# Attention kernel with exponentials on two engines: V by column tiles, the first K and Q in halves, one warm-up run, rearranged loads, new constants for the planner

## The chip, the cores and the metric

The kernel runs on one core of a Trainium2 chip. A core has TensorE (PE, matmuls; PEld is its weight load), VectorE (DVE), ScalarE (ACT), GpSimd (POOL), and SyncE (SP), which here only issues DMAs. They run beside each other and wait for each other by semaphores. The metric is the device time of one execution in microseconds, the median over several runs.

## What is computed

Two attention layers of 16 heads of 28 over 2048 positions of width 448; their outputs stand side by side in one 896-wide result. Layer A has one K and one V for all heads (softmax over all 2048 keys); layer B has its own K and V per head and looks at 8 keys, every second position backwards.

```python
def _A_ref(x, wq, wk, wv, wo):
    q = (x @ wq).reshape(B, S, H, Dh) with heads in front
    k = x @ wk
    v = x @ wv
    scores = jnp.einsum("bhqd,bkd->bhqk", q, k) * (Dh ** -0.5)
    p = _softmax(scores, axis=-1)
    o = jnp.einsum("bhqk,bkd->bhqd", p, v)
    return o (heads side by side) @ wo
def _B_ref(x, wqkv, wo):
    q, k, v = heads of (x @ wqkv)
    idx = pos[:, None] - 2 * arange(8)[None, :]
    logits = jnp.einsum("bhsd,bhswd->bhsw", q, k[idx]) * scale, -1e9 where idx < 0
    attn = _softmax(logits, axis=-1)
    o = jnp.einsum("bhsw,bhswd->bhsd", attn, v[idx])
    return o (heads side by side) @ wo
return jnp.concatenate([a, b], axis=-1)
```

## The kernel before

The program is recorded as a list of operations, each with an engine, an estimated duration, what it reads and writes, a priority `pr` (lower goes first) and sometimes an earliest time `rel`. A planner (`Sched.run`) plays them on a clock of its own, picks for each engine the ready operation with the lowest `pr`, and so fixes the order of each engine's instructions; `resolve` then derives the semaphore waits. On the chip the engines follow that order strictly: durations and `rel` shape the order and nothing else.

Layer A. The scores are computed transposed, 128 keys by 512 queries: a unit is (query block of 512 `sc`, group of four heads `t`, key tile `tb`, head in the group `j`), 4 x 4 x 16 x 4 = 1024 units. Units are taken three and two at a time in turn into PSUM banks 0 to 2 and 3 to 4 (`SLOTS`). For each such group PE computes the scores (QK, lines 808 to 816), and ScalarE takes the exponential of the whole group in one instruction (line 833, 1536 or 1024 wide). QK has two forms: tiled, where three or two matmuls of 28 (32) rows run beside each other in row tiles (line 816), or full, where each matmul uses the whole array on a K that is zero outside its head's rows (`kz`, line 813). The planner takes the full form where its running sum of PE activity is below a bound, and puts in matmuls on a zero tile (`warm`) as fillers (lines 413, 436 and 808) to keep that sum up. For a few groups a quad, VectorE takes one unit's exponential instead of ScalarE (`d_exp`: line 912 out of PSUM into `d_x`, then the polynomial of lines 921, 923 and 925 on 1024 columns; `OFF_AT` says in which rounds). PV (line 879) multiplies the exponentials by V for four heads at a time in column tiles into bank 5; V has a column with the softmax's denominator (`v_aug`). After a quad's 64 units VectorE transposes and divides (lines 939 to 948), and after four quads PE multiplies by the output matrix (line 962). Banks 6 and 7 (`XBANKS`) serve everything else.

The head (`a_head`, `a_tr`, `a_v`, `a_q`). PE runs `WARM` matmuls on zeros (line 651). The first two blocks of 512 rows of x come in plain and are transposed on PE (line 694) and copied out (lines 702 and 705); the other two come by DMA transposes on SP. K and Q of a block are matmuls of 512 columns (lines 660 and 752) in four steps over the width; then each is squared (line 666 on ScalarE for K's first block, 758 for the first Q, VectorE otherwise), the squares are multiplied by a constant matrix into the same bank (lines 674 and 766), so that three spare rows carry the softmax's shift, and VectorE copies the bank out with a constant added (lines 677 and 770). The first QK waits for both copies. V of a block is computed as x times wv in sixteen matmuls of 28 columns (line 716) into a bank of its own, beside four one-column matmuls (line 723), whose exponential (line 727, ScalarE, `gcol`) scales V (line 731).

Layer B goes through in 16 blocks of 128 positions between these: q, k (line 1003) and v (line 1018) on PE; v is stored to DRAM and loaded back shifted, eight times (lines 1025 and 1027 on SP); products on VectorE (1044 and 1098) and sums on PE (1053 and 1104); the softmax's exponential is on ScalarE (line 1079), 256 columns for two blocks. Its first positions need zero rows in DRAM, written at line 631.

## Time and profile before

| | us |
|---|---|
| median of the runs | 452.68 (452.05 to 453.52, 4 runs) |
| the profiled execution | 452.05 |
| its span, first to last instruction | 450.0 |
| first exponential of line 833 starts | 10.83 |
| ScalarE busy, of it line 833 | 435.2, 429.7 |
| VectorE busy | 416.8 |
| PE busy (weight loads) | 418.6 (164.1) |
| mean granted PE clock | 0.999 |

Busy time is the union of an engine's instructions; a row of groups shows the line, engine and operation, what is written from what, and, after the bars, busy us, mean ns of one, and the idle time just before, with who ended it. The order of the first DMAs is: SP issues wk, then eight transposes of A's x (4.55 to 14.86), wqkv, and all sixteen of B's x (16.10 to 41.40), and then the zero rows; ACT issues the first two blocks of x and the first part of wq; POOL issues wv (2.24 and 3.14), the rest of wq (7.66 and 8.43), B's wv (8.96 and 9.72) and the two output matrices (10.25 and 12.76).

### The profile page before, as it was taken

To read this page: it belongs to the slowest core of one execution; us is meant where nothing else is said; L and a number is where in the kernel's file an instruction comes from. 1 tells how busy PE (TensorE), PEld (TensorE's weight loads), DVE (VectorE), ACT (ScalarE), POOL (GpSimd) and SP (SyncE) were. 2 spreads that over 40 slices of the span, in tenths; PEclk is the share of its full clock that TensorE was granted. 3 is DMA by queue.
4 is the path that set the end of the run, shared out by engine and by line. 5 is a ranking of instruction groups with operands and counts; after the bars stand their busy time and mean duration, and the time that the engine had idled before them with its cause. 6 is when DMAs were issued, how large, how long until landed. Compare 5 with 4: busy or idle time off the path is not lost.

```text
span 450.0 us, 9035 instructions
## 1 busy us (share of the span) xinstructions
PE 418.6 (93%) x3806; PEld 164.1 (36%) x3806; DVE 416.8 (93%) x672; ACT 435.2 (97%) x429; POOL 14.4 (3%) x37
## 2 busy tenths in 40 slices
PE   8998999898999999999899999999999899998894
PEld 3332223232344324234362353324433244442441
DVE  6778999999998999999989999999999989799972
ACT  3998999999999999999999999999999999999995
POOL 8300000000000000000000000000000000000000
PEclk9999999999999999999999999999999999999999
DMA  7994022000023002002050240002300123330001
GB/s 168 224 111 82 15 79 93 12 1 1 16 89 114 32 20 84 21 13 82 14 172 31 65 152 12 12 0 94 104 12 11 42 83 103 97 98 1 12 1 52
DMA packets 39988, 27.30 MB, mean 61 GB/s; under 512 B 15518, under 2 KB 39592, under 8 KB 39948
## 3 DMA queue, kind: packets, MB, share of 16 engines
q1 hardware_dynamic: 37452, 24.06, 19.5%
q0 software_dynamic: 816, 1.53, 1.7%
q10 hardware_dynamic: 1680, 1.13, 0.8%
q8 instruction: 30, 0.49, 0.5%
q14 instruction: 10, 0.08, 0.1%
HBM read 18.06 MB, written 5.52 MB: 52 GB/s over the span
## 4 chain that ended last, share of the span: by engine, by line
ACT 91%; DVE 5%; PE 3%; POOL 1%; issue 0%; POOLq 0%
ACT expT L833 90%; PE ps L660 1%; DVE kz L680 1%; DVE d_x L912 1%; ACT e_t L1079 1%; DVE d_u L921 1%; DVE d_u L923 1%; DVE xT_A L702 0%; PE ps L813 0%; DVE qT L770 0%; DVE kT L677 0%; PE ps L436 0%; PE ps L816 0%; DVE kT L670 0%; DVE dexp L925 0%
## 5 line engine op out<-in xcount | busy, mean ns | idle before, releaser
L833 ACT ACTIVATE expT<-ps 128x1024 bf16<-128x1024 f32 (+1 forms) x410 | 429.7, 1257 | 4.3 <-PE ps L816 2.1
L816 PE MATMUL ps<-qT,kT 32*128 32x512 bf16 (+1 forms) x918 | 130.4, 372 | 13.7 <-ACT expT L833 10.6
L879 PE MATMUL ps<-expT,v_aug 128*32 128x512 bf16 (+1 forms) x1000 | 89.8, 375 | 1.4 <-ACT expT L833 1.0
L816 PEld LDWEIGHTS ps<-qT,kT 32*128 32x128 bf16 x918 | 32.8, 91 | 101.8 <-ACT expT L833 87.0
L912 DVE TENSOR_SCALAR d_x<-ps 128x512 f32<-128x512 f32 x84 | 57.4, 684 | 2.1 <-PE ps L816 1.9
L813 PE MATMUL ps<-qT,kz 128*128 128x512 bf16 (+1 forms) x170 | 47.1, 367 | 7.1 <-ACT expT L833 5.4
L925 DVE SCALAR_TENSOR_TENSOR dexp<-d_u,d_x 128x1024 int16<-128x1024 f32 x42 | 51.2, 1218 | 0.1
L923 DVE SCALAR_TENSOR_TENSOR d_u<-d_u,d_x 128x1024 f32<-128x1024 f32 x42 | 51.2, 1218 | 0.1
L921 DVE SCALAR_TENSOR_TENSOR d_u<-d_x 128x1024 f32<-128x1024 uint16 x42 | 51.1, 1216 | 0.2
L1044 DVE TENSOR_TENSOR stage<-qTB,kTB 112x1024 bf16<-112x1024 bf16 x64 | 42.3, 677 | 1.0 <-PE ps L1053 0.9
L1104 PE MATMUL ps<-ident,prod 128*112 128x128 bf16 x512 | 42.2, 224 | 0.0
L1098 DVE TENSOR_TENSOR prod<-Vsh,a_n 128x896 bf16<-128x896 bf16 x64 | 37.6, 616 | 4.7 <-PE ps L1104 4.7
L1003 PE MATMUL ps<-xT_B,wqkv 128*128 128x512 bf16 x128 | 39.0, 383 | 0.7 <-DVE qT L770 0.4
L879 PEld LDWEIGHTS ps<-expT,v_aug 128*32 128x32 bf16 x1000 | 22.1, 93 | 47.9 <-issue 43.1
L1104 PEld LDWEIGHTS ps<-ident,prod 128*112 128x112 bf16 x512 | 34.0, 129 | 14.7 <-issue 11.7
L1053 PEld LDWEIGHTS ps<-ones,stage 112*128 112x128 bf16 x512 | 19.9, 96 | 9.2 <-issue 4.3
L1053 PE MATMUL ps<-ones,stage 112*128 112x4 bf16 x512 | 22.9, 167 | 0.0
L752 PE MATMUL ps<-xT_A,wq 128*128 128x512 bf16 x64 | 19.6, 383 | 0.4 <-DVE kTB L1008 0.2
L813 PEld LDWEIGHTS ps<-qT,kz 128*128 128x128 bf16 x170 | 10.9, 97 | 24.0 <-ACT expT L833 21.1
L1018 PE MATMUL ps<-wqv,xT_B 128*128 128x448 bf16 x64 | 18.1, 356 | 0.9 <-DVE kTB L1008 0.5
L1111 PE MATMUL ps<-wo_B,oT 112*128 112x448 bf16 x64 | 18.3, 357 | 0.0
L962 PE MATMUL ps<-wo,oTn 128*128 128x448 bf16 x64 | 16.5, 355 | 1.1 <-DVE oTn L948 1.1
(105 smaller groups left out, 304.0 us busy)
## 6 DMA issues: line engine op xcount, KB each, us to landing
Vsh<-v_scratch SPq DMA_DIRECT2D x16, 896.0 KB, 4.7
v_scratch<-Vst SPq DMA_DIRECT2D x16, 112.0 KB, 1.7
out_dram<-outB SPq DMA_DIRECT2D x16, 112.0 KB, 1.7
out_dram<-outA SPq DMA_DIRECT2D x15, 112.0 KB, 1.7
stage<-in_A_x_dram ACTq DMA_DIRECT2D x2, 448.0 KB, 4.2
wqkv<-in_B_wqkv_dram SPq DMA_DIRECT2D x1, 672.0 KB, 9.6
wo_B<-in_B_wo_dram POOLq DMA_DIRECT2D x4, 98.0 KB, 5.9
wo<-in_A_wo_dram POOLq DMA_DIRECT2D x4, 98.0 KB, 6.7
```

The source lines that it names most:

```text
L813: r = e.matmul(g.bank(b0 + i, nq, nq * k), g.kz[:, j, 128 * tb:128 * tb + 128], g.qT[:, sc % 2, t, q0:q0 + nq], start=True, stop=True)
L816: r = e.matmul(g.bank(b0 + i, nq, nq * k), g.kT[32 * j:32 * j + 32, 128 * tb:128 * tb + 128], g.qT[32 * j:32 * j + 32, sc % 2, t, q0:q0 + ...
L833: x = a("act", t_exp(w), lambda e, b0=b0, w=w, n=n: e.activation(g.expT[:, n % ERING, 0:w], g.ps[:, 512 * b0:512 * b0 + w], ACT.Exp, scale ...
L879: x = e.matmul(g.bank(PVBANK, nq, q0, p0=32 * j, p1=32 * j + 32), g.v_aug[:, w, tb, :], src[:, nq * k:nq * k + nq], start=first, stop=last ...
L912: o = a("dve", t_dve_ps(512), lambda e: e.tensor_scalar(out=xx[:, 512 * h:512 * h + 512], in0=g.bank(bank), scalar1=-128.0 * A2, scalar2=1 ...
L921: a("dve", t_dve_1x(1024), lambda e: e.scalar_tensor_tensor(out=u, in0=lo, scalar=EP * F, in1=lo, op0=ALU.add, op1=ALU.mult), R=di, W=["d_ ...
L923: a("dve", t_dve_1x(1024), lambda e: e.scalar_tensor_tensor(out=v, in0=u, scalar=EQ * F * F, in1=lo, op0=ALU.add, op1=ALU.mult), R=["d_u"] ...
L925: a("dve", t_dve_1x(1024), lambda e: e.scalar_tensor_tensor(out=out, in0=v, scalar=EL / F ** 3, in1=xx, op0=ALU.mult, op1=ALU.subtract), R ...
L1003: a("pe", t_mm(512), lambda e, u=u, t=t, kt=kt, w=w: e.matmul(g.bank(u.bank), g.wqkv[:, kt, w * D + KC * t:w * D + KC * t + 128], g.xT_B[: ...
L1044: op = a("dve", t_dve_2x(1024), lambda e, t=t, qv=qv, kv=kv: e.tensor_tensor(out=g.prodT[0:KC, t, :, :], in0=qv, in1=kv, op=ALU.mult), R=R ...
L1053: r = e.matmul(g.bank(u.bank, 128).rearrange("p (h w) -> p h w", w=WIN)[:, 4 * t:4 * t + 4, w], g.prodT[0:KC, t, w, :], g.ones4[:, :], sta ...
L1104: a("pe", 0.056, lambda e, u=u, t=t, w=w: e.matmul(g.bank(u.bank, 128, 128 * t, p1=KC), g.prod2[:, w, KC * t:KC * t + KC], g.ident[:, :], ...
```

## The change

- V is computed transposed: per step over the width one group of four column tiles (32 columns each, `wv4` is wv padded to 32), 128 columns long, so 16 matmuls in four groups a block; VectorE transposes the bank (`vT`) and scales it out of SBUF. The one-column matmuls of line 723 now write into the bank of the block's K, which stays in use until their exponential is done.
- K's first block and the first Q are computed, squared, corrected and copied in two halves of 256 columns; the first QK's need only their own half of K (`key_of`). The copy of K's first half goes before the copies of x.
- The warm-up is one operation of eight matmuls and one of a single matmul.
- The zero rows come from the `warm` tile and are stored early on SP; the memset of `Vst` is gone. B's x is transposed in blocks as before, but blocks 2 and 3 stand later in SP's order. The rest of wq is issued earlier on POOL, B's wv and both output matrices later.
- `d_x` has three buffers instead of two, `outA` two instead of four; the polynomials have a priority by quad instead of a fixed one; in the first quad the offload begins in round 4 instead of 7.
- The planner's constants are new: window, bounds, the activity credited to tiled operations, and a small extra duration after a change of tiling mode.

On the engines' orders this gives 20 full QK groups instead of 76 (of 410), 35 single filler matmuls instead of 23, and 14 fillers inside other operations instead of 42. ScalarE keeps its exponentials: 288 of 1024, 121 of 1536 and one of 512.

```diff
-WARM = 9
+WARM = 8
+KF = 256
...
-OFF_AT[0] = (7, 8, 9, 10)
+OFF_AT[0] = (4, 5, 6, 7)
 LATE = 2
-PSTT = -1.5
+PSTT = -35.0
 DR = 2
+DX = 3
...
-    MODE = 0.09
+    MODE = 0.096
     NPV = 3
-    WIN = 2.2
-    WANT = 1200.0
-    IDLE = 1300.0
-    FULL = {2: 1500.0, 3: 1200.0}
-    LOW = 900.0
-    QKT = 0.315
+    WIN = 2.5
+    WANT = 1300.0
+    IDLE = 1400.0
+    FULL = {2: 1400.0, 3: 1300.0}
+    LOW = 1200.0
+    QKT = 0.32
...
+                elif mode and not o.tiled:
+                    o.dur += o.extra
...
-        self.outA = sb([128, 4, D], BF16, "outA")
+        self.outA = sb([128, 2, D], BF16, "outA")
...
+        a("dve", 0.1, lambda e: e.memset(g.wv4[:, :, :], 0.0), W=["wv4z"], pr=-6.5)
...
-        a("gp", 1.5, wload(g.wq, g.A_wq, KC, D), R=[("d_x", 0, 0), ("d_x", 0, 1)], W=[("wq", 1)], dsem="i_wq", land=4, pr=-7.5, ninc=2)
+        a("gp", 1.5, wload(g.wq, g.A_wq, KC, D), R=[("d_x", 0, 0), ("d_x", 0, 1)], W=[("wq", 1)], dsem="i_wq", land=5.5, pr=-8.15, ninc=2)
...
-                    transpose=True)), R=[("xst", 0)], W=[("xT_B", c, t)], dsem=f"i_xb{c}.{t}", land=4.5, pr=-16 + c)
+                    transpose=True)), R=[("xst", 0)], W=[("xT_B", c, t)], dsem=f"i_xb{c}.{t}", land=6.0, pr=-16 + c, rel=(0, 0, 60, 130)[c])
...
-        a("sp", 0.6, one(lambda e: e.dma_start(out=g.v_dram[0:PAD, :], in_=g.Vst[0:PAD, 0, :])),
-          R=[("Vst", 0)], W=[("vd", -1)], dsem="i_vz", land=2.5, pr=3, rel=4)
+        a("sp", 0.6, one(lambda e: e.dma_start(out=g.v_dram[0:PAD, :], in_=g.warm[0:PAD, 0:D])),
+          R=["warm"], W=[("vd", -1)], dsem="i_vz", land=2.5, pr=-24)
...
+        a("dve", 0.1, lambda e: e.tensor_copy(out=g.wv4[:, :, 0:DH], in_=g.wv[:, :, :]), R=["wv", "wvz", "wv4z"], W=["wv4"], pr=-5)
...
+        for n, pr, rel in ((WARM, -30, 0.0), (1, -15, 4.6)):
+            def warm(e, n=n):
+                for _ in range(n):
+                    r = e.matmul(g.bank(3), g.warm[:, 0:128], g.warm[:, :], start=True, stop=True)
+                return r
...
+            for k, (lo, n) in enumerate(((0, KF), (KF, 512 - KF)) if c == 0 else ((0, 512),)):
+                u = Use(f"K{c}.{k}", HB, late=c == 0)
...
-            g.a_v(c)
+            g.a_v(c, u)
...
+        u = Use(f"V{c}", g.LB)
+        for kt in range(4):
+            def vm(e, u=u, kt=kt):
+                for i in range(4):
+                    r = e.matmul(g.bank(u.bank, 128, 0, 32 * i, 32 * i + 32), g.wv4[:, kt, :],
+                                 g.xT_A[:, kt, 512 * c:512 * c + 512].rearrange("p (t i e) -> p i t e", t=4, e=32)[:, i],
+                                 start=kt == 0, stop=kt == 3, tile_position=(0, 32 * i))
+                return r
+            o = a("pe", 0.13, vm, R=[("xT", c, kt), "wv4"], W=[u], use=u, pr=pr, rel=11.0 if c == 0 else 0, dense=192)
+            o.tiled = True
+        a("dve", t_dve_ps(128), lambda e, u=u: e.transpose(out=g.vT[:, c % 2, :], in_=g.bank(u.bank, 128)),
+          R=[u], W=[("vT", c % 2)], use=u, pr=-2)
+        u = uk
...
+            for hf, (lo, n) in enumerate(((0, 256), (256, 256)) if first and t == 0 else ((0, 512),)):
+                pr += 0.1 * hf
+                u = Use(f"Q{sc}.{t}.{hf}", banks, late=first and t == 0)
...
-            o.dense = 128
+            o.dense = 256 + 32 * len(us)
...
-        xx, out = g.d_x[:, m % 2, :], g.dexp[:, m % DR, :]
+        xx, out = g.d_x[:, m % DX, :], g.dexp[:, m % DR, :]
...
+            pp = 10.0 + 26.7 * (4 * g.quad[0] + g.quad[1]) + PSTT
...
-            ob = blk % 4
+            ob = blk % 2
```

## The prediction

> **What bounds the kernel now.** I read the page first (engine shares, the chain that ended last), then ScalarE by shape, then its waits, then the timeline of the head, and last the stretches.
>
> ```profile
> PE 418.6 (93%) x3806; PEld 164.1 (36%) x3806; DVE 416.8 (93%) x672; ACT 435.2 (97%) x429; POOL 14.4 (3%) x37
> ...
> ACT 91%; DVE 5%; PE 3%; POOL 1%; issue 0%; POOLq 0%
> ```
>
> Three engines are above 90%, but the chain that ended last is 91% ScalarE: the exponentials of line 833, one behind the other. By shape:
>
> ```profile
> L833 ACT ACTIVATE expT<-ps 128x1024 bf16<-128x1024 f32 x288 | 291.6, 1134 | 2.1 <-PE ps L813 1.5 <-PE ps L879 0.7
> L833 ACT ACTIVATE expT<-ps 128x1536 bf16<-128x1536 f32 x121 | 188.3, 1556 | 2.1 <-PE ps L816 2.1
> ...
> L833 ACT ACTIVATE expT<-ps 128x512 bf16<-128x512 f32 x1 | 0.8, 767 | 0.0
> ```
>
> The means times the counts (288 x 1.134 + 121 x 1.556 + 0.8 = 516) exceed the 429.7 busy us of the group, so neighbours overlap by about 0.2 us each, and a wait shorter than that overlap never shows as idle. What does show is little, and where it lies is the point:
>
> ```profile
> 17.95 5.97 ACT L833 ACTIVATE expT<-ps 128x1536 bf16<-128x1536 f32 x5 [0.18 <-PE ps L816]
> ...
> 32.61 5.12 ACT L833 ACTIVATE expT<-ps 128x1024 bf16<-128x1024 f32 x5 [0.66 <-PE ps L879]
> 37.87 0.17 ACT L727 ACTIVATE gcol<-ps 128x4 f32<-128x4 f32 x1 [0.15 <-PE ps L723]
> 39.53 6.46 ACT L833 ACTIVATE expT<-ps 128x1024 bf16<-128x1024 f32 x6 [1.49 <-PE ps L813]
> ```
>
> This is ScalarE's timeline: start, length, and in brackets the idle time before. The four sum to 2.48 us, all before 40 us. The stretches (us; then busy time of PE, PEld, DVE, ACT, POOL; clock) agree that nothing is idle later:
>
> ```profile
> 31.95:39.53 7.58, 5.92 (x57) 2.33 (x61) 7.58 (x11) 5.29 (x6) 0.20 (x1) 1.00 0.51 83
> ...
> 45.00:100.00 55.00, 51.85 (x405) 16.47 (x403) 54.63 (x82) 55.00 (x55) 0.00 (x0) 1.00 0.13 41
> 100.00:200.00 100.00, 94.86 (x802) 34.71 (x799) 97.83 (x149) 100.00 (x99) 0.00 (x0) 1.00 0.13 43
> ...
> 444.30:450.00 5.70, 1.60 (x13) 0.42 (x13) 2.15 (x5) 0.54 (x1) 0.00 (x0) 0.88 0.12 40
> ```
>
> So the 450.0 us are a head of 10.83 (to the first exponential), a loop of 433.4 (to 444.2), and a tail of 5.8. The head ends like this:
>
> ```profile
> 8.59 0.75 DVE L770 TENSOR_SCALAR qT<-ps,cols 128x512 bf16<-128x512 f32 x1 [2.15 <-PE ps L766]
> 8.97 0.39 PE L674 MATMUL ps<-d_u,hq 128*128 128x512 bf16 x1
> 9.26 0.41 DVE L702 COPY xT_A<-ps 128x512 bf16<-128x512 bf16 x1
> 9.59 0.74 DVE L677 TENSOR_SCALAR kT<-ps,cols 128x512 bf16<-128x512 f32 x1
> 10.39 0.39 PE L816 MATMUL ps<-qT,kT 32*128 32x512 bf16 x3 [0.58 <-DVE kT L677]
> 10.83 5.97 ACT L833 ACTIVATE expT<-ps 128x1536 bf16<-128x1536 f32 x5 [1.91 <-PE ps L816]
> ```
>
> Q's and K's corrections are one 512-wide pass each, with a copy for the next x block between them on VectorE.
>
> **What the Trainium skill says.** "TensorE: Matmul & The Clock Gate", section "What's actually happening": the array runs at half rate until one free-running activity window of about 3.4 us was busy, and falls back after an idle one. The trace agrees: seven warm-up matmuls from 1.25 to 4.42 us at 0.43 us each, later ones at 0.21, and a granted clock of 0.88 in the thin last stretch. Same page, section "Measured speedup vs the span model": column tiles run beside each other (2.38 times for three). Four tiles of line 879 start together and the group takes 0.39 us, like one matmul. "TensorEngine Tiling", section "Key Properties": a change of tiling mode drains the array; at 10.71 and 11.03 us a weight load stands idle 0.23 us just at such changes. "DMA: Bandwidth & Descriptors", section "Issuing engines are not separate DMA queues": all queues share the 16 DMA engines, so what POOL issues earlier competes with ACT's loads; the stretch 10.83 to 18 shows a DMA share of 1.17.
>
> **The change part by part**, against the profiled run: 452.05 us, span 450.0, so 2.05 around it, which I keep. The median of the four runs shown is 452.68.
>
> *Head.* Warm-up: the old seven already run without a gap (7 x 0.43 = 3.0 of the 3.17), so one long run of eight brings no heat that was lacking; it ends near 1.25 + 8 x 0.43 = 4.69 instead of 4.42, and the transposes that began at 4.58 may lose 0.1. VectorE, busy from 3.2 to 6.4 us but for short issue gaps, gets one more small memset (0.1) and the wq copy (0.26) ahead of the x copies: the last x copy ends near 6.55 instead of 6.44, and Q's last matmul of the first half starts at 6.6. Halves of 256: pitch 0.11, end 6.87; ScalarE square (0.60 at 512; about 0.38 at 256) 6.93 to 7.31; hq matmul behind five K matmuls, 7.47 to 7.74; qT halves (0.75 at 512; about 0.43 at 256) 7.8 to 8.65; K's first half squared 7.6 to 8.0, its hq matmul behind two transposes to 8.45; kT first half 8.65 to 9.1, with no copy in between. QK needs only that half: 9.15, and the first exponential 0.45 later as before: 9.6. POOL's rest of wq (294 KB) is issued some 4 us earlier, beside the second x block, which landed at 2.72 + 4.7 = 7.4; its transposes stand in PE's queue ahead of K's hq matmul at 8.0. A slip of 0 to 1 us costs 0 to 0.4; I take 0.1. First exponential 9.7: minus 1.1 (bounds -1.4 to -0.5). The zero-row store is one issue (0.6) on SP ahead of transposes that wait for x at 4.55 anyway: nothing. wv4's copy waits on VectorE for wv (issued 3.14, 4.3 to land: 7.44), with qT queued behind it until 7.8: 0.3 of cover, and any slip beyond it goes one to one into the head.
>
> *Early loop.* Q's and K's halves take four banks (0 to 3), and K's last one is now kept for the column of line 723 and its exponential. The second pair's banks are 3 and 4, so its QK stands behind that small exponential; the order on ScalarE shows 1536, gcol, 1536, 1024: the third group overtakes the second. That third one needs the first exponential's banks: after it ends, a warm matmul (0.22), the QK (0.39) and the release (0.06) pass: idle 0.7. Second bubble: chunk 1's kT. VectorE has, from the end of kT's second half at 9.5, four x copies (4 x 0.36), three wq copies (0.8), four kz (4 x 0.36), vT (0.3 by the slope of STREAM_TRANSPOSE, 0.44 at 256 and 0.71 at 512), two v_aug (0.45), the K copy 0.68, the product 0.41, another vT, the hq matmul and 0.75: about 16.5, against 15.4 before. Chunk 0 lasts 16 of 5 units a round, 3.2 rounds of 2.23 us, plus the bubble: to 16.2. Idle 0.6 (0 to 1.5). The old four waits belong to K3, V's sixteen 28-wide matmuls a chunk with fillers, and Q of t=1 behind the offload's polynomials. V becomes four column-tile groups a chunk (16 x 0.13 = 2.1 us of PE for 64 x 0.06 + 13 fillers x 0.15 = 5.8), Q's copies get VectorE before the polynomials, and K3's, V3's and Q's products stand earlier in the order. I leave 0.4 for remnants. Sum 1.7 for 2.48: minus 0.8 (bounds -2.0 to +0.8). POOL's later loads of wqv, wo_B and wo free DMA in 10 to 18 us; B's late x waits on SP behind B's first V stores, 40 us or more before it is used: nothing.
>
> *Rest of the loop.* The order has 20 full-array QK groups instead of 76, 35 filler matmuls for 23, 14 inner fillers for 42, and 47 more entries into tiled mode. In PE time: 56 x 0.1 and 28 x 0.15 and V's 3.7 saved, 47 x 0.1 and 12 x 0.22 added: 6 us less of 418.6. PE was not the bound, and the clock was already 1.00. A loop without any wait would be about 424 (121 pairs at 2.23, 167 exponentials of 1024 at 0.90, eight of 0.3 for e_t), an estimate from the runs of exponentials above, so about 6 us of waits hidden under the overlap exist to be won or doubled. I take 0, with -1.5 to +2. DVE: a third d_x buffer and polynomials ordered by quad, 42 x 3 x 1.22 us unchanged: nothing unless a QK waits for its bank's reader, which is what these bounds hold. Two outA buffers: each is rewritten long after its 1.7 us store.
>
> *Tail.* The last exponential is 512 wide; three output matmuls (0.56) stand before the last PV and end about 0.1 after it: +0.1.
>
> Sum: -1.1 - 0.8 + 0 + 0.1 = -1.8. Profiled 450.25; median 452.68 - 1.8 = **450.9**.
>
> **Rivals.** *A, the head's gain is returned in the bubbles* (the same): if wv, wq or kT of chunk 1 are a microsecond later than worked out, -1.1 in the head stands against +0.8 in the loop: 452.4. For it: the two new bubbles are sure by bank and order. Against it: the old 1.49 and 0.66 lose their causes. *B, the clock falls* (slower): with full-array QKs gone, PE runs thin in places. The thinnest is after chunk 2's K matmuls: QK 3 and 2, one PV group, one hq, QK 2, so five streams of 512 (2560 columns) while ScalarE works some 3.3 us, a third of full rate. Before shows 1.00 at a PE busy share of 5.92/7.58 and a fall at 1.60/5.70; a third lies near the fall. One half-rate window of 3.4 us puts 1.7 us of PE work late, and beside a PE at 97% it is not caught up. It decides from two windows in a run: -1.8 + 3.4, so 454.3. Against it: the windows are free-running, so a short thin patch seldom fills one. *C, the hidden waits shrink* with the lighter PE: -1.5 more, 449.4; this is the low end of my forecast.
>
> **How the numbers follow.** This kernel's runs spread by 0.3%, so 0.2% (0.9 us) is about what can be told from no change. Forecast with C 0.66, A 0.17, B 0.17. The range: 449.0 (C and a slightly better head) to 453.0 (A with 0.6 above it); B is left out but for its edge. Faster (below 451.8) 0.68 with the lower edge of A; same 0.14; slower (above 453.6) 0.18.
>
> **What would show it.** First exponential at 9.4 to 10.0; a 0.7 idle behind the first exponential, another near 16.5; no idle at 32 and 38; 100.00 of 100 us busy later; clock 1.00 to the tail, and QK matmuls of 0.39 in every stretch. Wrong would be a first exponential after 10.4, matmuls of 0.6 in mid-loop, or a loop from first to last exponential above 433.4.

## The result, and the profile after

The changed kernel takes 451.13 us in the median of 43 runs (449.21 to 466.87), the kernel before 452.68 in 64; the ratio is 0.996, with a 95% interval of 0.9948 to 0.9972. Ratios leave out slow runs, more than 1.5% above the fastest of their kernel: here the four from 456.76 on, further down the two above 500 of experiment 2 and the two longest of experiment 4. The forecast was 450.9. The profiled run took 451.95 us, with a span of 450.2.

The median hides something. The 43 runs do not scatter, they stand on steps, and the mean granted clock of TensorE stands on the same steps:

| runs | time, us | mean clock |
|---|---|---|
| 12 | 449.21 to 449.75 | 0.996 to 0.998 |
| 12 | 450.57 to 451.60 | 0.992 to 0.995 |
| 6 | 451.94 to 452.01 | 0.990 to 0.991 |
| 9 | 452.95 to 453.60 | 0.987 to 0.988 |
| 4 | 456.76 to 466.87 | 0.976 and below |

A stretch of 3.41 us at half rate lowers the mean clock of a 450 us run by 3.41 x 0.5 / 450 = 0.004, so one step is one such stretch. The kernel before has steps too, of about 0.6: its fastest runs, at 452.04 to 452.13, have a clock of 0.998 or 0.999, those around its median, near 452.6, one of 0.996. Its traced run, at 452.05, is of the fastest, so where the clock falls in the others is not on record.

The changed kernel's profiled run is of the third group and has two stretches. Its page first: busy time by engine, the clock in 40 slices, and the chain that ended last.

```profile
PE 419.3 (93%) x3800; PEld 159.0 (35%) x3800; DVE 419.3 (93%) x680; ACT 435.2 (97%) x431; POOL 14.0 (3%) x36
...
PEclk9999999999999999999999989989999999999999
...
ACT 94%; PE 3%; POOL 1%; DVE 1%; issue 0%; POOLq 0%
```

The chain is still ScalarE, one exponential behind the other. What is new are the two slices with an 8 in the clock, the 24th and the 27th, in mid-loop. ScalarE's timeline (start, length, idle time before in brackets), first the early loop:

```profile
10.06 1.45 ACT L864 ACTIVATE expT<-ps 128x1536 bf16<-128x1536 f32 x1 [1.18 <-PE ps L847]
11.41 0.17 ACT L754 ACTIVATE gcol<-ps 128x4 f32<-128x4 f32 x1
12.33 4.62 ACT L864 ACTIVATE expT<-ps 128x1536 bf16<-128x1536 f32 x4 [0.75 <-PE ps L847]
17.44 2.36 ACT L864 ACTIVATE expT<-ps 128x1024 bf16<-128x1024 f32 x2 [0.49 <-PE ps L847]
...
31.64 18.89 ACT L864 ACTIVATE expT<-ps 128x1024 bf16<-128x1024 f32 x18
```

The waits at 18, 32, 38 and 39 us are gone, two new ones stand at 12.33 and 17.44, and no other follows up to 50. The same view in the middle, where before had no idle time:

```profile
265.20 1.02 ACT L864 ACTIVATE expT<-ps 128x1024 bf16<-128x1024 f32 x1 [0.41 <-PE ps L844]
266.72 1.02 ACT L864 ACTIVATE expT<-ps 128x1024 bf16<-128x1024 f32 x1 [0.49 <-PE ps L844]
...
296.12 1.02 ACT L864 ACTIVATE expT<-ps 128x1024 bf16<-128x1024 f32 x1 [0.51 <-PE ps L844]
297.63 1.02 ACT L864 ACTIVATE expT<-ps 128x1024 bf16<-128x1024 f32 x1 [0.49 <-PE ps L844]
```

ScalarE waits for full-array QK matmuls. The stretches (start and end, length, then busy time of PE, PEld, DVE, ACT, POOL, then the clock) say why:

```profile
45.00:100.00 55.00, 53.06 (x415) 16.15 (x413) 54.65 (x82) 55.00 (x55) 0.00 (x0) 1.00 0.12 29
100.00:200.00 100.00, 95.35 (x844) 36.33 (x842) 98.13 (x149) 100.00 (x99) 0.00 (x0) 1.00 0.21 58
...
260.79:264.20 3.41, 2.64 (x27) 1.06 (x27) 3.41 (x7) 3.41 (x4) 0.00 (x0) 1.00 0.30 91
264.20:267.61 3.41, 3.41 (x20) 1.48 (x18) 3.04 (x6) 2.51 (x3) 0.00 (x0) 0.50 0.63 212
...
291.51:294.92 3.41, 2.36 (x15) 0.69 (x15) 3.41 (x7) 3.41 (x5) 0.00 (x0) 1.00 0.00 0
294.92:298.33 3.41, 3.41 (x11) 0.69 (x9) 2.00 (x5) 2.41 (x3) 0.00 (x0) 0.50 0.00 0
```

Each half-rate stretch is exactly 3.41 us long and follows a stretch of the same length in which PE was busy 2.64 or 2.36 us. PE did not stop for a whole window there; it ran tiled matmuls with gaps, the longest 0.62 and 0.90 us. In the half-rate stretches a full-array matmul of 512 columns takes 0.61 to 0.63 us instead of 0.38, and ScalarE falls from 3.41 busy to 2.51 and 2.41.

Waits shorter than the overlap of two exponentials never show as idle time. To count them too, I took every pair of neighbours on ScalarE and set the distance of their starts against the pace back to back (0.904 us for 1024 columns, 1.331 for 1536, and 0.05 and 0.30 for a small exponential of `gcol` or `e_t` between two, from the runs of exponentials in the trace). What is above that pace, by place:

| us lost | before | after, profiled |
|---|---|---|
| first exponential starts | 10.83 | 10.06 |
| up to 20 us | 0.39 | 1.61 |
| 20 to 45 us | 3.01 | 0.13 |
| after 45 us | 5.34 | 7.50, of it 1.78 and 1.74 in the two half-rate stretches |
| last exponential's end to the span's end | 5.75 | 5.96 |

The head gained 0.77 and the early loop 3.40 - 1.74 = 1.66, and the tail lost 0.21. If the two stretches' 3.52 were simply taken out, the loop after 45 us would have gained 5.34 - 3.98 = 1.36. The runs say less. Those at 449.22, which have no stretch in the loop, have a span of 447.5, against 450.0 of before's traced run, which has none either: 2.5 gained, so 0.3 is left for the loop after 45 us. (The trace of experiment 1, without a stretch too, loses 4.82 there, 0.5 less than before.) And the runs with two stretches stand 2.73 above those with none (451.95 against 449.22), not 3.52: part of what a stretch costs in place is won back later. How is not shown.

So undisturbed against undisturbed the gain is 452.05 - 449.22 = 2.8 us, of which 0.3 lies outside the span (2.05 around it before, 1.7 now). In the median run 1.9 of it is given back. Before's median in turn stands 0.6 above its undisturbed runs, so that the medians differ by 1.55.

### The profile page after: what moved, and what is told of

Same layout as the page of the kernel before. It is cut to its first block, busy times and chain, and to the rows that moved or that the text cites. A ratio compares the mean times of both kernels' runs of the same rounds, so it can differ in the third digit from the quotient of the medians.

```text
span 450.2 us, 9037 instructions
## 1 busy us (share of the span) xinstructions
PE 419.3 (93%) x3800; PEld 159.0 (35%) x3800; DVE 419.3 (93%) x680; ACT 435.2 (97%) x431; POOL 14.0 (3%) x36
## 4 chain that ended last, share of the span: by engine, by line
ACT 94%; PE 3%; POOL 1%; DVE 1%; issue 0%; POOLq 0%
ACT expT L864 93%; PE ps L844 1%; ACT e_t L1111 1%; PE ps L847 1%; PE ps L994 0%; PE ps L910 0%; PE ps L781 0%; DVE qT L800 0%; POOL wqkv L572 0%; POOL wv L601 0%; PE ps L1136 0%; POOL d_x L601 0%; PE ps L796 0%; POOL wv L602 0%; PE ps L675 0%
## 5 line engine op out<-in xcount | busy, mean ns | idle before, releaser
L847 PE MATMUL ps<-qT,kT 32*128 32x512 bf16 (+1 forms) x1043 | 151.8, 371 | 18.1 <-ACT expT L864 13.3
L910 PE MATMUL ps<-expT,v_aug 128*32 128x512 bf16 (+1 forms) x1000 | 95.2, 377 | 0.0
L847 PEld LDWEIGHTS ps<-qT,kT 32*128 32x128 bf16 x1043 | 37.9, 91 | 116.7 <-ACT expT L864 104.8
L1136 PE MATMUL ps<-ident,prod 128*112 128x128 bf16 x512 | 46.4, 227 | 0.1
L910 PEld LDWEIGHTS ps<-expT,v_aug 128*32 128x32 bf16 x1000 | 24.1, 93 | 53.3 <-issue 50.4
L1035 PE MATMUL ps<-xT_B,wqkv 128*128 128x512 bf16 x128 | 40.3, 386 | 0.1
L1085 PEld LDWEIGHTS ps<-ones,stage 112*128 112x128 bf16 x512 | 18.6, 96 | 10.0 <-issue 5.9
L781 PE MATMUL ps<-xT_A,wq 128*128 128x512 bf16 (+1 forms) x68 | 20.3, 371 | 0.3 <-DVE wq L645 0.3
L844 PE MATMUL ps<-qT,kz 128*128 128x512 bf16 (+1 forms) x45 | 14.5, 418 | 2.9 <-ACT expT L864 2.7
L971 DVE STREAM_TRANSPOSE PV_T<-ps 128x512 f32<-128x512 f32 (+1 forms) x17 | 11.6, 681 | 5.8 <-PE ps L910 5.7
```

The source lines that it names most:

```text
L847: r = e.matmul(g.bank(b0 + i, nq, nq * k), g.kT[32 * j:32 * j + 32, 128 * tb:128 * tb + 128], g.qT[32 * j:32 * j + 32, sc % 2, t, q0:q0 + ...
L910: x = e.matmul(g.bank(PVBANK, nq, q0, p0=32 * j, p1=32 * j + 32), g.v_aug[:, w, tb, :], src[:, nq * k:nq * k + nq], start=first, stop=last ...
L1035: a("pe", t_mm(512), lambda e, u=u, t=t, kt=kt, w=w: e.matmul(g.bank(u.bank), g.wqkv[:, kt, w * D + KC * t:w * D + KC * t + 128], g.xT_B[: ...
L1085: r = e.matmul(g.bank(u.bank, 128).rearrange("p (h w) -> p h w", w=WIN)[:, 4 * t:4 * t + 4, w], g.prodT[0:KC, t, w, :], g.ones4[:, :], sta ...
L1136: a("pe", 0.056, lambda e, u=u, t=t, w=w: e.matmul(g.bank(u.bank, 128, 128 * t, p1=KC), g.prod2[:, w, KC * t:KC * t + KC], g.ident[:, :], ...
```

## Experiments

Twelve kernels. Where nothing else is said, a diff is against the first experiment, which is the changed kernel with fillers enough to keep the clock in most runs, so that half-rate stretches blur the rest less.

**1. Is it the clock-keeping?** The changed kernel with the planner's old window and bounds and the old credit for QK and PV (its durations stay the new ones). The edit touches the rules for filler and full-array matmuls only, but the planner then orders everything anew: of VectorE's 678 instructions that can be compared 239 stand at the same place as in the changed kernel, of ScalarE's 430 all but 16.

```diff
-    WIN = 2.5
-    WANT = 1300.0
-    IDLE = 1400.0
-    FULL = {2: 1400.0, 3: 1300.0}
-    LOW = 1200.0
+    WIN = 2.2
+    WANT = 1200.0
+    IDLE = 1300.0
+    FULL = {2: 1500.0, 3: 1200.0}
+    LOW = 900.0
...
-            o.dense = 256 + 32 * len(us)
+            o.dense = 128
...
-            {(k, y[3], z[0] // 4) for k in ("v_aug", "v_aug1") for y in grp for z in g.parts(y[0])}), pr=-40, dense=768)
+            {(k, y[3], z[0] // 4) for k in ("v_aug", "v_aug1") for y in grp for z in g.parts(y[0])}), pr=-40, dense=700)
```

> The changed kernel with the old activity rules alone (WIN 2.2, WANT 1200, IDLE 1300, FULL 1500/1200, LOW 900, a tiled QK credited with 128 and a PV with 700 columns); head, V, loads and priorities stay changed, and the order has 69 full QK groups instead of 20. Theory clock: the changed kernel loses what lies above 449.2 us to windows of 3.41 us at half clock, about 1 to 1.7 us each, which come where the array streams too little. With the old rules there are none: 449.2 to 449.8, clock 0.998 in every run, no QK or PV of 0.6 us, and first exponential at 10.0 to 10.1 as in the changed kernel. Theory late PE: the half-rate windows only go along with QKs that are late because tiled groups were taken for cheaper than they are; with the full groups back PE is as full as before and the hidden waits return: 450.5 to 451.5.

Measured: 449.43 (449.41 to 451.24, 7 runs), ratio 0.9938 [0.9916, 0.996]. Five of the seven lie within 0.11 us of each other; the other two, at 451.15 and 451.24, have a clock of 0.994 and so a stretch each, which I had not expected. The stretches of its trace at the same two places:

```profile
264.20:267.61 3.41, 3.41 (x38) 1.81 (x36) 3.41 (x5) 3.41 (x5) 0.00 (x0) 1.00 0.40 129
294.92:298.33 3.41, 3.41 (x26) 1.23 (x25) 3.41 (x6) 3.41 (x4) 0.00 (x0) 1.00 0.00 0
```

Full clock, ScalarE without a gap, and no other half-rate stretch in the loop. The steps of the changed kernel are the half-rate stretches, and its order with the new constants has far more of them: 31 of 43 runs have one, against 4 of the 40 of experiments 1, 3, 5, 6 and 10, which all have the old constants. The constants alone do not keep the clock: experiments 4 and 9 have the old ones too, and at least 16 of the 22 runs of the one and seven of the 14 of the other have a stretch. What counts is the order that comes out of them.

**2. No clock-keeping at all.** The changed kernel with every bound at zero, so that the planner puts in no fillers for the clock and chooses no full-array QK for it.

```diff
-    WANT = 1300.0
-    IDLE = 1400.0
-    FULL = {2: 1400.0, 3: 1300.0}
-    LOW = 1200.0
+    WANT = 0.0
+    IDLE = 0.0
+    FULL = {2: 0.0, 3: 0.0}
+    LOW = 0.0
```

> The changed kernel with all bounds of the activity rules at zero: no filler matmul and no full QK group at all, nothing else changed; PE has some 17 us less to do. Theory clock: ten to fifteen windows of 3.41 us at half clock, each 1.0 to 1.7 us late: 460 to 475 us, clock 0.94 to 0.96, and matmuls of 0.6 us in stretches that begin on a grid of 3.41 us. Theory late PE: less work on PE leaves fewer late QKs: 448 to 449.5, with a clock not below 0.99.

Measured: 489.5 and 490.85, with clocks of 0.859 and 0.854, and 502.8 and 504.94, with 0.825 and 0.819; the median of the four is 496.82, and the ratio 1.0825 [1.0783, 1.0868] is that of the first two. The profile is of the 504.94. The sign is the clock theory's; the size is far above what I gave it. The late-PE theory, which had 448 to 449.5 here, is refuted; what less work on PE would be worth at full clock can't be seen in this kernel. Its page (clock by slice) and one of its stretches:

```profile
PEclk9879985999557555897999999998969895575886
```

```profile
161.06:205.43 44.37, 44.33 (x272) 13.23 (x268) 30.19 (x50) 31.43 (x30) 0.00 (x0) 0.50 0.12 38
```

44.37 us at half rate, thirteen windows of 3.41, with PE busy from end to end and ScalarE busy 31.43. PE's busy time is full, and still the clock does not come back. A fall can last.

**3. The bubble behind the first exponential.** The four one-column matmuls go into V's bank instead of K's, so that bank 3 is free once kT is copied.

```diff
-        u = uk
...
-                g.bank(u.bank, 1, b), g.kT[0:32, 128 * tb:128 * tb + 128], g.e30[:, :], start=True, stop=True),
+                g.bank(u.bank, 1, 128 + b), g.kT[0:32, 128 * tb:128 * tb + 128], g.e30[:, :], start=True, stop=True),
...
-        a("act", 0.2, lambda e, u=u: e.activation(gc, g.bank(u.bank, 4), ACT.Exp, scale=SCALE),
+        a("act", 0.2, lambda e, u=u: e.activation(gc, g.bank(u.bank, 4, 128), ACT.Exp, scale=SCALE),
```

> As e1_oldthr, but the one-column matmuls of line 750 go into columns 128 to 131 of V's own bank instead of the bank of K, so that bank 3 is free once kT's second half is copied. Theory banks: the idle 0.75 us behind the first exponential comes from bank 3 being held until the column's exponential is done; here the second exponential follows the first without idle time, and the idle time before 20 us is below 0.4. V's banks are held longer instead, and about 0.7 to 1.0 of idle time is expected near 38: 449.0 to 449.6. Rival: the idle time has another cause (the overtaking third group, the filler in front of it) and stays at 0.7: then 449.5 to 450.3, since the wait near 38 comes on top.

Measured: 449.21 (448.96 to 449.46, 6 runs), ratio 0.9921 [0.99, 0.9941]. ScalarE's timeline:

```profile
10.13 4.63 ACT L863 ACTIVATE expT<-ps 128x1536 bf16<-128x1536 f32 x4 [1.19 <-PE ps L846]
14.65 0.18 ACT L753 ACTIVATE gcol<-ps 128x4 f32<-128x4 f32 x1
...
39.47 6.03 ACT L863 ACTIVATE expT<-ps 128x1024 bf16<-128x1024 f32 x6 [0.82 <-PE ps L909]
```

Four exponentials, 1536 and 1024 wide in turn (the row names the shape of the first), run on from the first, so the bank was the cause of the 0.75. The second bubble, 0.49 at 17.44, goes with it. In the changed kernel it looks like this:

```profile
16.04 0.75 DVE L692 TENSOR_SCALAR kT<-ps,cols 128x512 bf16<-128x512 f32 x1 [0.65 <-PE ps L689]
...
17.00 0.11 PEld L847 LDWEIGHTS ps<-qT,kT 32*128 32x128 bf16 x5 [0.63 <-ACT expT L864]
17.01 0.60 PE L847 MATMUL ps<-qT,kT 32*128 32x512 bf16 x5
...
17.44 1.02 ACT L864 ACTIVATE expT<-ps 128x1024 bf16<-128x1024 f32 x1 [0.49 <-PE ps L847]
```

K of chunk 1 (`kT`) is there at 16.79. What released QK at 17.00 is an exponential of 1024 that ended at 16.95, just before this one of 1024, on the same two banks: once the third group has overtaken the second, two of these stand one behind the other. In experiment 3 the widths alternate, kT is there at 16.79 too, and this is what is left, a wait for kT:

```profile
16.84 0.10 PEld L846 LDWEIGHTS ps<-qT,kT 32*128 32x128 bf16 x3 [0.52 <-DVE kT L692]
...
17.28 2.37 ACT L863 ACTIVATE expT<-ps 128x1536 bf16<-128x1536 f32 x2 [0.18 <-PE ps L846]
```

Another wait of 0.82 appears at 39 us, as expected, and the gain over experiment 1 is 0.2.

**4. The loads.** The changed kernel with the old order of the loads (and the planner's old constants). The diff shows a part; `Vst`'s memset on POOL is back too.

```diff
-        a("gp", 1.5, wload(g.wq, g.A_wq, KC, D), R=[("d_x", 0, 0), ("d_x", 0, 1)], W=[("wq", 1)], dsem="i_wq", land=5.5, pr=-8.15, ninc=2)
+        a("gp", 1.5, wload(g.wq, g.A_wq, KC, D), R=[("d_x", 0, 0), ("d_x", 0, 1)], W=[("wq", 1)], dsem="i_wq", land=4, pr=-7.5, ninc=2)
...
-          R=["warm"], W=[("vd", -1)], dsem="i_vz", land=2.5, pr=-24)
+          R=[("Vst", 0)], W=[("vd", -1)], dsem="i_vz", land=2.5, pr=3, rel=4)
...
-          W=["wqv"], dsem="i_wbv", land=8, pr=-7, rel=15, ninc=2)
+          W=["wqv"], dsem="i_wbv", land=5, pr=-7, ninc=2)
```

> As e1_oldthr, with the loads as in the kernel before (rest of wq late on POOL, B's wv and the output matrices early, zero rows from Vst after all of B's x). Theory neutral: the moved loads hide nothing on the path, 449.2 to 449.8, first exponential 9.9 to 10.1. Rival collision: the early rest of wq takes DMA time from the second x block, whose transposes stand before K's correction on PE, so undoing it brings the first exponential 0.1 to 0.4 earlier; or the early POOL loads slow the transposed x of block 2 and K of block 2 waits for a DMA between 15 and 17: later by 0.3 to 1.

Measured: 453.2 (450.18 to 458.45, 22 runs), ratio 0.9994 [0.9979, 1.0009]. This doesn't price the loads: the moved loads change the whole order, its profiled run has half-rate stretches at 46.06 and 383.98, and its times scatter as after's do. What it does show is a head 0.30 shorter (9.76). The cause is on VectorE and POOL. The timeline of the changed kernel:

```profile
3.74 0.77 POOL L601 DMA_DIRECT2D d_x<-in_A_wq_dram  x1
4.51 0.55 POOL L602 DMA_DIRECT2D d_x<-in_A_wq_dram  x1
5.04 0.87 POOL L572 MEMSET wqkv<- 64x896 bf16 x1
5.21 0.84 DVE L640 COPY wk<-wk 128x448 bf16<-128x448 bf16 x1
5.96 0.30 DVE L645 COPY wq<-d_x 128x448 bf16<-128x448 bf16 x1
6.18 0.73 DVE L725 COPY xT_A<-ps 128x512 bf16<-128x512 bf16 x2
```

and of experiment 4:

```profile
5.01 0.47 POOL L574 MEMSET wqv<- 64x448 bf16 x1
5.20 0.40 DVE L641 COPY wk<-wk 128x448 bf16<-128x448 bf16 x1
```

In both, wk's copy ends 0.12 to 0.14 us after the memset that was running when it began (6.05 against 5.91; 5.60 against 5.48), while wq's copy of the same shape takes 0.26 to 0.30. All 14 traces agree: in the nine with the long memset there wk's copy takes 0.83 or 0.84, in the five with the short one 0.38 to 0.51, and it always ends 0.12 to 0.14 behind the memset. The copy waits for POOL. wq's rest, issued from 3.74 to 5.06 on POOL, pushed POOL's longest memset from 3.9 to 5.04, beside wk's copy.

**5 and 6. wq's rest issued late, alone.** The same kernel twice.

```diff
-        a("gp", 1.5, wload(g.wq, g.A_wq, KC, D), R=[("d_x", 0, 0), ("d_x", 0, 1)], W=[("wq", 1)], dsem="i_wq", land=5.5, pr=-8.15, ninc=2)
+        a("gp", 1.5, wload(g.wq, g.A_wq, KC, D), R=[("d_x", 0, 0), ("d_x", 0, 1)], W=[("wq", 1)], dsem="i_wq", land=4, pr=-7.5, ninc=2)
```

> As e1_oldthr, with the rest of wq issued on POOL after the memsets, as in the kernel before; from the second exponential on the order is the same but for a few DVE and PE places before 13 us. Theory port: in the changed kernel the copy that spreads wk (line 640) takes 0.84 instead of 0.51 us because POOL's memset of wqkv (line 572), pushed later by the two issues of wq, runs at the same time; here the copy takes 0.40 to 0.52, the first exponential starts at 9.7 to 9.8 instead of 10.1, and the kernel takes 449.1 to 449.2 against 449.4. Theory DMA: the early wq delays the second x block; then the copy stays at 0.84 and the first exponential comes earlier only where PE's transposes at 8.4 no longer wait. Rival: the 0.3 us comes back as a longer wait for chunk 1's K near 16, 449.4.

> The kernel m_wqlate again, since its first exponential at 10.46 came with a first full-rate window at 7.02 us, against 6.11 in e1_oldthr and 4.78 in the changed kernel, so that head and clock were mixed. Theory port: the copy of wk again takes 0.38 to 0.41 us, and where full rate begins before 6.2 us the first exponential is at 9.7 to 9.9; the time is 449.1 to 449.4 in such runs. Rival: the copy's 0.45 us are not on the path, and the first exponential is at 10.0 or later whatever the clock.

Measured: 449.84 (449.72 to 450.22, 5 runs), ratio 0.9941 [0.9929, 0.9954], and 449.76 (449.06 to 451.8, 11 runs), ratio 0.9925 [0.9896, 0.9955], against 449.43 for experiment 1. wk's copy takes 0.39 in both, as it should, and with full rate early, in the second, the first exponential comes at 9.60, a little before the 9.7 to 9.9 of the port theory. Yet nothing is gained in the time: only three of the 11 runs of experiment 6 lie below 449.4. In the first profile PE came to full rate at 7.02 us only, and the first exponential at 10.46. In the second, full rate came at 4.19 and the first exponential at 9.60; then this (VectorE's and ScalarE's timeline):

```profile
13.34 0.46 DVE L645 COPY wq<-d_x 128x448 bf16<-128x448 bf16 x2 [1.91 <-DMA d_x<-in_A_wq_dram]
...
14.42 0.31 DVE L745 STREAM_TRANSPOSE vT<-ps 128x128 f32<-128x128 f32 x1
```

```profile
15.39 2.37 ACT L864 ACTIVATE expT<-ps 128x1536 bf16<-128x1536 f32 x2 [1.17 <-PE ps L847]
```

VectorE stands 1.91 us at wq's copy, whose load came late; V's transpose is queued behind it, PE's V matmuls behind that, and QK behind those. The early issue buys cover for this and pays with the memset.

**7. K and Q in one piece.**

```diff
-KF = 256
+KF = 512
...
-            for hf, (lo, n) in enumerate(((0, 256), (256, 256)) if first and t == 0 else ((0, 512),)):
+            for hf, (lo, n) in enumerate(((0, 512),)):
```

> As e1_oldthr, with K's first block and the first Q whole again (one 512-wide pass each). Theory halves: the first exponential comes at 10.7 to 10.9, 0.7 later than with halves, since the correction, square and copy are one 0.6 to 0.75 us step each again; the idle time behind the first exponential does not go with them, and the kernel takes 450.2 to 450.9. Rival: what the halves gain in the head is given back behind the first exponential, so undoing them costs nothing: 449.3 to 449.7.

Measured: 451.72 (451.56 to 455.16, 15 runs), ratio 0.9983 [0.997, 0.9996]: 2.3 above experiment 1, more than I had given it. The first exponential starts at 11.28 instead of 10.13, and the early loop changes its order with it: idle times of 0.43 and 0.91 us come back at 22.49 and 32.29 (2.20 lost between 20 and 45, by the count of the table above, for 0.34). In this profile full rate came at 6.88, in experiment 1's at 6.11, so not all of the 1.15 is the halves'.

**8. V by sixteen matmuls a block in a bank of its own, as before.** The edit also moves the one-column matmuls into V's bank and gives V its old place in the order (a priority of 1.3 for 0.5); the diff shows a part.

```diff
...
-            o = a("pe", 0.13, vm, R=[("xT", c, kt), "wv4"], W=[u], use=u, pr=pr, rel=11.0 if c == 0 else 0, dense=192)
-            o.tiled = True
-        a("dve", t_dve_ps(128), lambda e, u=u: e.transpose(out=g.vT[:, c % 2, :], in_=g.bank(u.bank, 128)),
-          R=[u], W=[("vT", c % 2)], use=u, pr=-2)
...
+        u = Use(f"V{c}", g.LB, spare=160)
+        for b in range(4):
+            tb = 4 * c + b
+            for kt in range(4):
+                o = a("pe", 0.07, lambda e, u=u, b=b, tb=tb, kt=kt: e.matmul(
+                    g.bank(u.bank, DH, 32 * b), g.xT_A[:, kt, 128 * tb:128 * tb + 128],
+                    g.wv[:, kt, :], start=kt == 0, stop=kt == 3),
...
```

> As e1_oldthr, with V of a block computed as before, sixteen matmuls of 28 columns and a bank of its own with the one-column matmuls. Theory V: the column tiles take some 3.7 us of PE out of the first 37 us, and this is what removed the idle 0.66 and 1.49 us of the kernel before near 32 and 38; with the old V more than 1 us of idle time comes back between 20 and 40, while the 0.75 behind the first exponential goes because bank 3 is free: together 449.8 to 450.8. Rival priorities: the waits near 32 and 38 went because Q's copies now go before the polynomials; then the idle time from 20 to 40 stays below 0.5 and the kernel is as fast or faster, 448.7 to 449.4.

Measured: 451.49 (451.36 to 452.38, 16 runs), ratio 0.9977 [0.997, 0.9985]: 2.1 above experiment 1, more than I had given it. ScalarE's timeline has the old pattern again:

```profile
23.58 0.17 ACT L750 ACTIVATE gcol<-ps 128x4 f32<-128x4 f32 x1 [0.52 <-PE ps L746]
...
30.36 0.17 ACT L750 ACTIVATE gcol<-ps 128x4 f32<-128x4 f32 x1 [0.41 <-PE ps L746]
30.98 1.02 ACT L860 ACTIVATE expT<-ps 128x1024 bf16<-128x1024 f32 x1 [0.44 <-PE ps L843]
32.83 4.62 ACT L860 ACTIVATE expT<-ps 128x1536 bf16<-128x1536 f32 x4 [0.82 <-PE ps L906]
```

These are waits for V's chain and the QK behind it. V as it is in the changed kernel removes them; what of it the column tiles do and what V's earlier place in the order does was not separated.

**9. The offload's rounds in the first quad, as before.**

```diff
-OFF_AT[0] = (4, 5, 6, 7)
+OFF_AT[0] = (7, 8, 9, 10)
```

> As e1_oldthr, with the first quad's offload in rounds 7 to 10 as in the kernel before instead of 4 to 7. Theory place: the polynomials of the first quad then fall on Q of t=1 to 3, and ScalarE waits for the second quad's QK near 38 for 1.5 to 2.5 us, as the kernel before did (1.49 idle): 451 to 452. Rival: with V by column tiles and Q's copies ahead of the polynomials this place no longer matters: 449.3 to 449.8.

Measured: 452.8 (452.54 to 455.35, 14 runs), ratio 1.0003 [0.9978, 1.0028]: 3.4 above experiment 1. That is more than I had given it, but at least seven of the 14 runs have a half-rate stretch. Six without one, at 452.54 to 452.56 with a clock of 0.997 or 0.998, stand 3.1 above experiment 1, and that is the price of this part, the largest of one part. ScalarE's timeline:

```profile
37.97 1.45 ACT L864 ACTIVATE expT<-ps 128x1536 bf16<-128x1536 f32 x1 [0.64 <-PE ps L844]
41.10 4.20 ACT L864 ACTIVATE expT<-ps 128x1024 bf16<-128x1024 f32 x4 [1.68 <-PE ps L844]
```

2.3 us of idle time are where before had its 0.15 and 1.49, and one half-rate stretch at 36.42 lies on them; how much of the 1.68 is that stretch's can't be read off this trace.

**10. Seven warm-up matmuls instead of eight.**

```diff
-WARM = 8
+WARM = 7
```

> As e1_oldthr, with seven matmuls in the warm-up run instead of eight (3.0 instead of 3.4 us of heat). Theory nothing: the head is the same within the place of the first full-rate window, 449.2 to 449.9. Rival heat: the eighth carries the array over to the transposes; without it the first full-rate window comes one window (3.4 us) later in some runs, and these runs are 0.5 to 1 us longer, with a first exponential after 10.6.

Measured: 449.44 (449.4 to 451.1, 11 runs), ratio 0.9923 [0.9897, 0.9948]; the first exponential starts at 10.06. The eighth matmul is worth nothing that can be seen.

**11. The same number of full groups, placed by another measure.** The changed kernel, with a tiled matmul credited by its share of the array (a QK of two at 256, PV at 512), and bounds that leave 21 full groups for after's 20.

```diff
-    WANT = 1300.0
-    IDLE = 1400.0
-    FULL = {2: 1400.0, 3: 1300.0}
-    LOW = 1200.0
+    WANT = 1200.0
+    IDLE = 1250.0
+    FULL = {2: 1200.0, 3: 1100.0}
+    LOW = 1000.0
...
-            o.dense = 256 + 32 * len(us)
+            o.dense = 128 * len(us)
```

> The changed kernel with the activity credited by the share of the array that a matmul fills (tiled QK 128 columns a unit, PV 512, V group 128, 98 and 10 for B's sums) and bounds WANT 1200, IDLE 1250, FULL 1200/1100, LOW 1000; the order keeps 21 full QK groups (20 in the changed kernel), 31 single fillers (35) and has 37 inner fillers for 14. Theory clock, in the form that the traces so far give (windows of 3.41 us that stream less than about 850 full-array columns a us turn into a half-rate window, 35% of full): nearly the same filling work at other places removes the half-rate windows in most runs: 449.2 to 449.8, a median at clock 0.997 or above, at most one run in five with a half-rate window. Theory full groups: it is the 49 more full QK groups of e1_oldthr that keep the clock, so with 21 the spread of the changed kernel stays, median 450.5 to 451.5.

Measured: 449.67, ratio 0.9925 [0.9901, 0.995]. Six of 13 runs lie at 449.09 to 449.19, one at 449.67, six at 450.48 to 450.84. The last six have a clock of 0.993 or 0.994. So no run has more than one half-rate stretch, where 19 of after's 43 have two or more, with as few full groups: it is not the 49 more full groups of experiment 1 alone that keep the clock. The order has 37 fillers inside other operations for 14, though, so whether their place or their number helps is not separated. And six runs of thirteen still have a stretch, more than I had expected; the measure is not sharp.

**12. The parts that helped, together.** Against experiment 1: the column matmuls in V's bank (experiment 3), wq's rest late but with the planner told its true landing time (5.5 instead of 4), V earlier in the order, and LOW at 850.

```diff
-    LOW = 900.0
+    LOW = 850.0
...
-        a("gp", 1.5, wload(g.wq, g.A_wq, KC, D), R=[("d_x", 0, 0), ("d_x", 0, 1)], W=[("wq", 1)], dsem="i_wq", land=5.5, pr=-8.15, ninc=2)
+        a("gp", 1.5, wload(g.wq, g.A_wq, KC, D), R=[("d_x", 0, 0), ("d_x", 0, 1)], W=[("wq", 1)], dsem="i_wq", land=5.5, pr=-7.5, ninc=2)
...
-    VPR = 0.5
-    VP0 = 0.5
+    VPR = 0.3
+    VP0 = 0.1
```

> A version put together from the findings: old activity rules (LOW 850), the column of line 749 in V's bank, the rest of wq late on POOL, V's priority 0.3 and 0.1 instead of 0.5. Both theories add up here: first exponential at 9.7 to 9.8, idle time before 45 us below 0.7 instead of 1.3, no half-rate window: 448.2 to 448.8. Rival: one half-rate window now and then (the thinnest stretch of the order lies just at the share where the clock fell), 449.3 to 450.3 in such runs.

Measured: **447.98** (447.49 to 448.32, 4 runs), ratio 0.9897 [0.9884, 0.9911]; it beats both kernels. ScalarE's timeline:

```profile
10.36 4.63 ACT L863 ACTIVATE expT<-ps 128x1536 bf16<-128x1536 f32 x4 [0.88 <-PE ps L846]
...
14.96 2.37 ACT L863 ACTIVATE expT<-ps 128x1536 bf16<-128x1536 f32 x2
17.51 2.36 ACT L863 ACTIVATE expT<-ps 128x1536 bf16<-128x1536 f32 x2 [0.18 <-PE ps L846]
...
33.05 17.54 ACT L863 ACTIVATE expT<-ps 128x1024 bf16<-128x1024 f32 x17
```

The time is below what I had expected, although the first exponential came later, at 10.36 for 9.7 to 9.8; full rate began only at 7.09 in this profile. From the first exponential on 0.18 us of idle time are left in the loop. VectorE now does V's first transpose (13.39) before wq's copies (13.63), so the wait of experiment 6 is gone. The four edits were not tried one by one beyond experiments 3, 5 and 6.

Not tried: four `outA` buffers again, and the third `d_x` buffer and the new polynomial priorities apart from the rest.

## Why the prediction was right

The number, -1.8 to 450.9, holds within 0.23 us, and that is luck. Undisturbed the change gains 2.8, one more than forecast, chiefly because the early loop's term was too small. The half-rate stretches, which the sum put at nothing, take 1.9 of it back in the median run, and before's median, from which the forecast starts, has 0.6 above its own undisturbed runs. The traced run, forecast at 450.25, took 451.95. Of the three signs of being wrong that the prediction named two came in it: full-array matmuls of 0.61 to 0.63 us in mid-loop, and 434.2 us from the first exponential to the end of the last, above 433.4. Point by point:

- *Head: first exponential at 9.7.* It was 10.06: -0.77 for -1.1, inside the bounds. The step that failed is "the last x copy ends near 6.55": it ended at 6.91. From there on the working holds: the first exponential follows the last x copy by 3.15 us in after, 3.19 in experiment 4 and 3.17 in experiment 6. I had counted wq's early issue against DMA time and not against POOL's own order, where it pushes a memset beside wk's copy. The Trainium skill, "SBUF — State Buffer", section "SBUF: two separate sides", states that GpSimd and a VectorE instruction in a two-port mode share a port pair that one of them holds for a whole instruction while the other blocks; the trace agrees (wk's copy 0.84 for 0.40, ending 0.14 behind the memset), though it does not show the copy's mode.
- *Warm-up: at most 0.1.* Right (experiment 10).
- *Two new bubbles, 0.7 and 0.6.* The first is right in size and cause: 0.75, and experiment 3 confirms the bank. The second is 0.49, but not for the cause given: QK did not wait for chunk 1's K, which was there at 16.79, but for the two banks of the exponential before it, until 16.95 (experiment 3). The sum for it does not hold either: a first exponential at 9.7, 3.2 rounds of 2.23 and a bubble of 0.7 end at 17.5, not at 16.2, and with a kT at 16.5 that leaves no wait. That the size came near was luck.
- *The old four waits go, 0.4 remain: -0.8.* The direction is right, and experiments 8 and 9 show that the new way and place of V and the offload's rounds are what removes them (2.1 and 3.1 us come back, together more than the 2.48 of visible idle time, so the two prices do not add). The term is too small: the early loop as a whole gained 1.66. I priced visible idle time only; before lost 3.01 between 20 and 45 us by the pace of the exponentials, of which 2.30 showed, and 0.13 was left of it, not 0.4.
- *Rest of the loop: 0.* In undisturbed runs it gained 0.3 to 0.5; with the profiled run's two stretches it lost 2.2. So 0 was near for the waits and wrong for the clock. Rival C's 1.5 more from hidden waits did not come: that undisturbed runs stand near its 449.4 is the early loop's doing. PE's busy time did not fall by the 6 us worked out: it is 419.3 for 418.6, of it about 3.4 from the two half-rate stretches, an estimate from their 6.82 us of full PE time at half rate.
- *Tail: +0.1.* It was +0.2.
- *Rival B.* Its price of 1.7 was right in place (1.74 to 1.78 us a stretch); in the runs the steps are 1.8, 0.95 and 1.05 apart, less than 1.7 from the second on. Its place was wrong (not behind chunk 2's K matmuls, but at 264 and 295 in the profiled run), and so was the argument against it, that a short thin patch seldom fills a window: with some 130 windows in a run it takes one that does, and 31 of the 43 runs have at least one. It should not have been a rival with 0.17 but a term of the sum, near +1.9.
- *Rival A.* The head's gain was not returned in the bubbles. The two bubbles are there, and the early loop gained in spite of them.

So the changed kernel is worth 2.8 us undisturbed, and the order that the new clock constants give costs 1.7 to 1.9 of it in the median run: experiment 1, which undoes only these, runs at 449.43, and the undisturbed runs of the changed kernel at 449.22.

## What to carry to other kernels

Where one engine runs back to back, compare the distance of its instructions' starts with its own pace, not only the idle time: of the 8.7 us that the kernel before lost by its own pace, 2.5 showed as idle. When times of one kernel fall on steps, look at the clock before anything else, and treat filler that keeps a clock as paid by the worst window, not by the mean. Of an instruction moved earlier on a queue, ask what it pushes later there, and beside what that then runs.

## What the runs showed of the hardware

- Half rate does not need a PE that is idle for a whole window. The Trainium skill, "TensorE: Matmul & The Clock Gate", section "What's actually happening", names an idle window of about 3.4 us as the cause. The window's length agrees (stretches between changes of the clock are multiples of 3.413 us in every trace), the cause does not: PE was busy 2.64 and 2.36 of 3.41 us in the two windows before the falls, with tiled matmuls and gaps of at most 0.62 and 0.90.
- Over 1769 full-rate windows in 14 traces, 31 were followed by half rate, ten of these wholly behind the last exponential. I counted the columns that PE streams in each window, as far as the traces record matmuls, a tiled matmul by its share of the array. Below about 765 columns per us every window fell, above about 975 none did, whether a matmul on a window's edge is split or counted where it starts; between the two both happened (in after, with splitting, 821 and 840 fell, 843 and 876 held). The best single threshold misplaces 6 to 11 windows by this count, and 15 by PE's busy time. What the chip really counts stays open.
- Half rate can last although PE is busy throughout: 44.37 us on end in experiment 2. In the loops of the other profiles it ended after one window. By the same count, with splitting, the half-rate windows that were followed by another streamed 436 to 906 columns per us, and those that ended it 788 to 1119.
- With a warm-up that began at 1.25 or 1.26 us (eight matmuls, seven in two of the kernels), full rate began at anything from 4.18 to 7.09 us in the 14 profiles. Experiments 5 and 6 are the same kernel: full rate at 7.02 goes with a first exponential at 10.46, at 4.19 with 9.60. Of these 0.86 us a wait of 0.38 for wq, in front of its copy, is another cause; how much is the clock's alone is not shown.
